# A linear-attention and mixture-of-experts kernel: rows of h scattered by expert and rank and gathered per unit, statistics and gate per unit

## The chip, the cores and the metric

The kernel runs on one core of one Trainium2 chip. A core has five engines with instruction streams of their own: TensorE (PE, matrix products), VectorE (DVE), ScalarE (ACT), GpSimd (POOL) and SyncE (SP, which here only starts DMA transfers). Each engine works its stream in order; semaphores tie the streams together. Sixteen DMA engines move data between HBM and SBUF; a transfer is started from SP's queue or, where the rows' addresses are data (indirect), from GpSimd's. The metric is the device time of one execution in microseconds.

## The reference

The input x has 2048 tokens of 512 numbers. Two blocks follow each other, each with a layer norm ahead of it and its input added to its result.

- Linear attention: q, k and v are products with wqkv; in each of 32 heads of 16, q and k go through a small matrix w_phi, and the features are softmax(p) and softmax(-p), 32 a head. With kv = phi_k^T v and z = the sum of phi_k, the output is (phi_q kv) / (phi_q z + 1e-6), times wo. So h = x + attention.
- A mixture of 8 experts, one a token: the logits are LN(h) w_gate, the largest one chooses the expert, and the token gets silu(LN(h) w1[e]) w2[e]. w1[e] is 512 x 1792, w2[e] 1792 x 512. The gate is a softmax over the one chosen logit, which is 1; both kernels compute it.

All numbers are 32-bit floats. With the given inputs the experts get 103, 594, 80, 127, 286, 222, 239 and 397 tokens.

## The kernel before, in words

**Precision.** Each large product is made of three on PE (`mm3`, L74 to L77): both operands are split into a high part (a rounded copy, by ScalarE, `hi_of`, L69) and a low part (what the rounding left, by VectorE, `lo_of`, L72). Weights are split in pieces by `split_chunk` (L170), whose subtraction (L176) goes to VectorE, or to GpSimd (`G`) where a tuple says so.

**Phase A** (`for c in range(NT - 1)`, L409) makes, per tile of 128 tokens, the layer norm, the k, q and v products, the features and the running kv. The gate's weights ride along with v and wo as extra columns, so that the logits of a tile come out of the same products; the mean is taken out afterwards with column sums of w_gate (`csg`, L366, L367, L471).

**Phase B** (`for c in range(NT + 8)`, L557) goes over the 16 tiles again, as a pipeline by hand: `s_num` (attention's quotient for tile c, L261), `s_ot` (transposed and split, c - 1), `s_wo` (output projection, residual, statistics and logits of h, c - 2), and by batches of two tiles `s_top` (the chosen expert as a one-hot row, running counts `cum`, the gate; L473), `s_rank` (each token's rank within its expert, L499) and `s_inv` (L525). h is written to a DRAM buffer `hbuf` in token order with mean, rstd and gate in extra columns (L497). `s_rank` and `s_inv` build an inverse table `ivf`: with two one-hot matrices and a product on PE (`acc`) each batch adds "token + 1" at (slot, expert and block of 128).

**Units.** A unit is 128 slots of one expert. The expert that leads after half the tokens, `star`, comes first; the others follow in order. Here that is 5 units for expert 1, then 1, 1, 1, 3, 2, 2 and 4: 19 units. In the middle of phase B `s_star` chooses the first expert and starts its seven weight chunks of 1 MB (`first_expert`, L178); when half the tokens have ranks, `s_first` reads the first unit's tokens from the table and gathers its rows (`gather`, L138). The splits of its first four chunks are laid into tiles 12 to 15 (L588), ten of sixteen low parts on GpSimd; `gemm1(0, ...)` (L594) is laid into the tail of the loop.

`unit(u)` (L719) then does: first product in four column groups (`g1`), silu, transposes and splits (`tr`), second product `g2` (14 steps into `py`), gate and residual (L797), indirect write of the rows to the output (L798). `prework(u + 1)` (L142) normalises the next unit's rows with the mean and rstd that came with them, transposes and splits them. `split(u, c)` splits a new expert's chunk under a run-time condition and then starts the load of the expert after it (`fetch`). In unit 0 stand `tables()` (L639: which unit has which expert, flags, and by `index`, L707, each unit's tokens from `ivf`), the splits of chunks 4 to 6 and the first loads for the next expert.

**What sets the order.** The source gives a priority; the framework's planner orders each engine's instructions by it and by when it expects their inputs, and may move a ready one ahead. A conditional block is moved as a whole. `issue_after` ties instructions behind a given one. So in a unit that splits, the next expert's chunks 0 to 2 are split while the unit's own first product runs, as each chunk comes free.

## Time and profile before

| | |
|---|---|
| median of 3 runs | 733.38 us (732.79 to 736.72) |
| profiled execution | 732.92 us |
| its span, first to last instruction | 731.2 us |
| VectorE / ScalarE / GpSimd busy | 468.8 / 303.2 / 180.8 us |
| DMA | 87.61 MB, mean 120 GB/s |

The span has five parts: the start to 12 us, phase A to some 205 us, phase B to some 310 us with the first unit laid into its end, the rest of the first unit to 336 us, and 18 units to 724 us, followed by the last write.

In the profile a busy time is the union of an engine's instructions. An idle time belongs to the instruction that ended it, with the instruction that released it behind the arrow. Durations of pipelined instructions overlap: where the next starts before one ends, the distance between starts is the cost. `out<-in` names what an instruction writes and reads, L is its line, x its count; "granted clock" is the share of PE's full clock.

### The profile page before, as it was taken

The numbers are of one execution on the slowest core, as the hardware profiler recorded it, in microseconds if no ns is written. First come the engines' busy times: TensorE is split into PE (matmuls) and PEld (weight loads), VectorE is DVE, ScalarE is ACT, GpSimd is POOL, SyncE is SP. The second block draws the span as 40 slices with busy tenths as digits, with TensorE's granted clock in tenths as the row PEclk, the third lists the DMA queues.
The fourth block names the chain that finished last, engine by engine and source line by source line (L and its number), as shares of the span: only waits on it lengthen the run. The fifth ranks groups of instructions, "written<-read, shape, count | busy, mean of one in ns | idle before, by whom it ended". The sixth has DMA issues, their size and how long they took to land.

```text
span 731.2 us, 12523 instructions
## 1 busy us (share of the span) xinstructions
PE 702.0 (96%) x4130; PEld 612.2 (84%) x4130; DVE 468.8 (64%) x969; ACT 303.2 (41%) x458; POOL 180.8 (25%) x281
## 2 busy tenths in 40 slices
PE   6999999999999998779999999999999999999996
PEld 6899999999989997658888888888888878888885
DVE  4996987878787889794512999972185472922211
ACT  4534444434322015152112888862274463822211
POOL 3364645434313328521110011110011111011110
PEclk9999999999999999899999999999999999999999
DMA  9111101100002249417400799981066381001000
GB/s 332 57 30 44 30 15 30 30 15 1 1 16 73 74 156 341 153 34 294 193 29 2 258 369 376 344 345 53 30 210 241 121 328 31 11 29 30 30 30 6
DMA packets 21912, 87.61 MB, mean 120 GB/s; under 512 B 3070, under 2 KB 3582, under 8 KB 14656
## 3 DMA queue, kind: packets, MB, share of 16 engines
q1 hardware_dynamic: 18624, 76.86, 28.8%
q0 software_dynamic: 3200, 9.75, 4.0%
q8 instruction: 34, 0.56, 0.3%
q14 instruction: 54, 0.44, 0.2%
HBM read 78.18 MB, written 9.21 MB: 120 GB/s over the span
## 4 chain that ended last, share of the span: by engine, by line
issue 46%; PE 35%; DMA 10%; DVE 6%; POOL 1%; ACT 1%; POOLq 1%; SPq 0%; DVEq 0%
DMA out_dram<-yo,sidx 8%; PE kvps L372 4%; PE pn L267 3%; PE pq L75 2%; PE pq L77 2%; PE pq L76 2%; PE ptq L381 2%; PE pv L77 2%; PE pv L76 2%; PE pv L75 2%; PE pk L75 2%; PE pk L77 2%; PE pk L76 2%; PE po L75 2%; PE po L76 2%
## 5 line engine op out<-in xcount | busy, mean ns | idle before, releaser
L69 ACT ACTIVATE whi<-raw 128x1024 fp32r<-128x1024 f32 (+1 forms) x120 | 118.7, 1003 | 67.9 <-PE mh L77 37.4
L176 DVE TENSOR_TENSOR wlo<-raw,whi 128x1024 fp32r<-128x1024 f32 (+1 forms) x110 | 130.6, 1200 | 18.6 <-ACT whi L69 12.5
L75 PE MATMUL mh<-whi,xhi 128*128 128x512 f32 (+1 forms) x304 | 114.9, 378 | 0.0
L77 PE MATMUL mh<-whi,xlo 128*128 128x512 f32 (+1 forms) x304 | 111.5, 367 | 0.0
L76 PE MATMUL mh<-wlo,xhi 128*128 128x512 f32 (+1 forms) x304 | 111.4, 366 | 0.0
L798 POOL DMA_INDIRECT out_dram<-yo,sidx x19 | 21.5, 1131 | 352.5 <-DVEq L635 202.0
L76 PE MATMUL my<-wlo,hThi 128*128 128x512 f32 x266 | 104.7, 393 | 3.5 <-DVE wlo L176 3.3
L75 PE MATMUL my<-whi,hThi 128*128 128x512 f32 x266 | 106.0, 399 | 0.3 <-ACT hThi L69 0.3
L77 PE MATMUL my<-whi,hTlo 128*128 128x512 f32 x266 | 104.6, 393 | 0.3 <-DVE hTlo L72 0.3
L72 DVE TENSOR_TENSOR hTlo<-mtr,hThi 128x512 fp32r<-128x512 f32 x76 | 47.0, 621 | 86.2 <-ACTq L635 53.3
L163 ACT ACTIVATE hs<-mh 128x512 f32<-128x512 f32 x76 | 41.0, 540 | 145.3 <-PE mh L77 145.3
L355 POOL TENSOR_TENSOR ph<-t,sm 128x1024 f32<-128x1024 f32 x32 | 62.1, 1939 | 66.9 <-DVE sm L353 37.8
L77 PEld LDWEIGHTS mh<-whi,xlo 128*128 128x128 f32 x304 | 57.2, 188 | 10.2
L76 PEld LDWEIGHTS mh<-wlo,xhi 128*128 128x128 f32 x304 | 57.3, 189 | 9.3
L75 PEld LDWEIGHTS mh<-whi,xhi 128*128 128x128 f32 x304 | 57.2, 188 | 9.3
L797 DVE SCALAR_TENSOR_TENSOR yo<-my,xg 128x512 f32<-128x512 f32 x19 | 14.2, 748 | 78.4 <-PE my L77 78.4
L76 PEld LDWEIGHTS my<-wlo,hThi 128*128 128x128 f32 x266 | 50.3, 189 | 14.2 <-DVE wlo L176 4.3
L77 PEld LDWEIGHTS my<-whi,hTlo 128*128 128x128 f32 x266 | 50.3, 189 | 11.2 <-DVE hTlo L72 0.5
L75 PEld LDWEIGHTS my<-whi,hThi 128*128 128x128 f32 x266 | 50.4, 189 | 10.5 <-ACT hThi L69 0.5
L352 DVE TENSOR_REDUCE sm<-t 128x64 f32<-128x1024 f32 x32 | 38.8, 1214 | 12.0 <-ACT t L347 11.9
L727 PE MATMUL mtr<-ident,hs 128*128 128x128 f32 x266 | 41.7, 274 | 2.7 <-DVE hTlo L72 2.6
L347 ACT ACTIVATE t<-t 128x1024 f32<-128x1024 f32 x32 | 33.9, 1061 | 20.9 <-DVE t L346 19.8
(206 smaller groups left out, 1407.3 us busy)
## 6 DMA issues: line engine op xcount, KB each, us to landing
raw<-in_w_dram SPq DMA_DIRECT2D x56, 1024.0 KB, 5.2
xt<-in_x_dram SPq DMA_DIRECT2D x32, 256.0 KB, 2.7
hbuf<-hb SPq DMA_DIRECT2D x8, 516.0 KB, 3.8
phT<-in_wqkT_dram SPq DMA_DIRECT2D x4, 512.0 KB, 5.1
phT<-in_wv_dram SPq DMA_DIRECT2D x2, 512.0 KB, 6.4
phT<-in_wo_dram SPq DMA_DIRECT2D x2, 512.0 KB, 8.2
phT<-in_woT_dram SPq DMA_DIRECT2D x2, 512.0 KB, 5.6
xg<-hbuf,gidx POOLq DMA_INDIRECT x21, 3.7
```

The source lines that it names most:

```text
L69: A.activation(dst, src, AF.Copy)
L72: V.tensor_tensor(dst, src, hi.bitcast(F32), op=OP.subtract)
L75: T.matmul(ps, ahi, bhi, start=first, stop=False)
L76: T.matmul(ps, ahi, blo, start=False, stop=False)
L77: T.matmul(ps, alo, bhi, start=False, stop=last)
L163: A.activation(hs[c % 2][:, 0:fw], p[:, 0:fw], AF.Silu)
L176: eng.tensor_tensor(wlo[c][:, w], raw[c][:, w], whi[c][:, w].bitcast(F32), op=OP.subtract)
L347: A.activation(t, t, AF.Exp)
L352: V.tensor_reduce(sm, t, AX.X, OP.add)
L355: G.tensor_tensor(ph.rearrange("p (a f) -> p a f", f=DH), t, bc(sm, DH), op=OP.mult)
L372: T.matmul(kvps[g // 4][:, g % 4, :], ph[:, g * P:(g + 1) * P], vt[:, 4 * g:4 * g + 4, :].rearrange("p h f -> p (h f)"), start=(c == 0 and ...
L727: T.transpose(pt[:, j * P:(j + 1) * P], hs[c % 2][:, j * P:(j + 1) * P], ident)
```

## The change

- `hbuf` has room for 2048 rows for each expert. A row holds h, the largest logit and the token's number. The running counts start at 2048 times the expert, so a token's rank is its row in `hbuf`; `s_rank` ends with that row number, and each tile is scattered from GpSimd's queue (`send`). The inverse table, `s_inv`, `index` and the one-hot matrices go. A unit's rows lie one after the other, and `gather` waits for all scatters issued before it.
- In phase A, 14 writes on SP's queue first fill all of `hbuf` with rows whose token number is out of range, so that empty slots write nothing.
- The gate's weights lose their column mean beforehand (`wgc`), so logits need no mean, and `s_wo` makes no statistics. The 1e-6 is added in halves to the two rows of z in `kvbd` (`epsz`).
- `stats(u)` makes mean, rstd and gate of a unit's rows after the gather: VectorE and GpSimd by turns. It stands after the first column group of the unit before.
- All low parts are VectorE's. The 16 pieces of chunks 0 to 3 are laid into tiles 12 to 17.
- Of the first unit only the first column group is laid ahead. Its tables are cut in two: row numbers first, so that `gather(1)` and `gather(2)` follow, flags later; the splits of chunks 4 to 6 stand between the products. Buffers of the units are allocated in another order.

```diff
-    hbuf = dram.tile([S, ROW], F32, name="hbuf")
+    hbuf = dram.tile([E * S, ROW], F32, name="hbuf")
...
+    def send(c, rows, hrow):
+        i = G.indirect_dma_start(out=hbuf, out_offset=bass.IndirectOffsetOnAxis(ap=rows, axis=0),
+                                 in_=hrow, in_offset=None)
+        for other in sent + fetched:
+            tc.declare_no_dep(i.ins, other.ins, reason="other rows of hbuf")
+        sent.append(i)
+
     def gather(u):
-        G.indirect_dma_start(out=xg[u % 3], out_offset=None, in_=hbuf if u else hbuf[0:S // 2, :],
-                             in_offset=bass.IndirectOffsetOnAxis(ap=gidx[:, u:u + 1], axis=0))
+        i = G.indirect_dma_start(out=xg[u % 3], out_offset=None, in_=hbuf,
+                                 in_offset=bass.IndirectOffsetOnAxis(ap=gidx[:, u:u + 1], axis=0))
+        for other in sent:
+            tc.add_manual_dep(i.ins, other.ins.name, mybir.DependencyInfo(
+                mybir.DependencyClass.Sync, mybir.DependencyReason.DATA), reason="rows of hbuf")
+        fetched.append(i)
+
+    def stats(u):
+        g = xg[u % 3]
+        bs = small.tile([P, 6], F32, name="ubs")
+        V.bn_stats(bs, g[:, 0:D])
+        V.bn_aggr(norm[:, u, :], bs)
+        sc = small.tile([P, 6], F32, name="usc")
+        G.tensor_scalar(sc[:, 0:1], norm[:, u, 1:2], EPS, None, op0=OP.add)
+        G.tensor_tensor(norm[:, u, 1:2], sc[:, 0:1], nhalf, op=OP.pow)
+        xi = V.tensor_scalar(xn2[0], g[:, 0:D], norm[:, u, 0:1], norm[:, u, 1:2], op0=OP.subtract, op1=OP.mult)
+        G.tensor_copy(sidx[:, u:u + 1], g[:, D + 1:D + 2])
+        V.tensor_reduce(sc[:, 1:2], g[:, D:D + 1], AX.X, OP.max)
+        G.tensor_tensor(sc[:, 2:3], g[:, D:D + 1], sc[:, 1:2], op=OP.subtract)
+        G.tensor_tensor(sc[:, 3:4], sc[:, 2:3], norm[:, u, 1:2], op=OP.mult)
+        G.tensor_tensor(sc[:, 4:5], euler, sc[:, 3:4], op=OP.pow)
+        G.tensor_scalar(sc[:, 5:6], sc[:, 4:5], 0.0, None, op0=OP.add)
+        G.tensor_tensor(sc[:, 5:6], sc[:, 5:6], mone, op=OP.pow)
+        G.tensor_tensor(gate[:, u:u + 1], sc[:, 4:5], sc[:, 5:6], op=OP.mult)
+        return xi
 
...
     def prework(u):
-        g = xg[u % 3]
-        xi = V.tensor_scalar(xn2[0], g[:, 0:D], g[:, D:D + 1], g[:, D + 1:D + 2], op0=OP.subtract, op1=OP.mult)
         pt = bank("mtr")
...
-    LO = (V,) * NW
-
-    def split_chunk(c, lo=None, n=2):
-        for i in range(n):
+    def split_chunk(c, n=2, part=None):
+        for i in range(n) if part is None else (part,):
             w = slice(i * (CW // n), (i + 1) * (CW // n))
             hi_of(whi[c][:, w], raw[c][:, w])
-            eng = lo or LO[c]
-            eng = eng[i] if isinstance(eng, tuple) else eng
-            eng.tensor_tensor(wlo[c][:, w], raw[c][:, w], whi[c][:, w].bitcast(F32), op=OP.subtract)
+            lo_of(wlo[c][:, w], raw[c][:, w], whi[c][:, w])
 
...
-        V.memset(cum[0], 0.0)
-        V.memset(ivf, 0.0)
+        G.iota(cum[0], pattern=[[S // P, E]], base=0, channel_multiplier=0, allow_small_or_imprecise_dtypes=True)
...
-                V.tensor_scalar(den, nv[:, :, DH:DH + 1], 1e-6, None, op0=OP.add)
-                V.reciprocal(den, den)
+                V.reciprocal(den, nv[:, :, DH:DH + 1])
                 V.tensor_tensor(o[:, 16 * i:16 * i + 16, :], nv[:, :, 0:DH],
...
+            V.tensor_scalar(csg, pc[:, 0:E], 1.0 / D, None, op0=OP.mult)
+            V.tensor_tensor(wgc, wgs, mid(csg, KD), op=OP.subtract)
...
+            def s_blank(c):
+                n = E * S // (NT - 2) // P
+                lo, hi = c * n * P, min((c + 1) * n * P, E * S) if c < NT - 3 else E * S
+                n = (hi - lo) // P
+                nc.sync.dma_start(hbuf[lo:hi, :].rearrange("(p r) f -> p r f", p=P),
+                                  blank.to_broadcast([P, n, ROW]))
...
-            ln_rstd(h[:, 0:D], h[:, D:D + 2], h[:, D + 1:D + 2])
-            V.scalar_tensor_tensor(lg, csg, h[:, D:D + 1], lg, op0=OP.mult, op1=OP.subtract)
...
-            G.tensor_tensor(hb[:, :, D + 2:D + 3], gt[:, 1], nr, op=OP.mult)
-            nc.sync.dma_start(hbuf[b * NB * P:(b + 1) * NB * P, :].rearrange("(c p) r -> p c r", p=P), hb)
...
-            rk = work.tile([P, NB], F32, name="rk")
-            V.tensor_reduce(rk, rs, AX.X, OP.add)
-            bs = work.tile([P, NB], F32, name="rb")
-            V.tensor_scalar(bs, rk, 0.25 - P / 2, FLOOR, op0=OP.add, op1=OP.add)
-            V.tensor_scalar(bs, bs, FLOOR, None, op0=OP.subtract)
-            sl = work.tile([P, NB], F32, name="sl")
-            V.tensor_tensor(sl, rk, bs, op=OP.subtract)
-            am = work.tile([P, NB, P], F16, name="am")
-            bm = work.tile([P, NB, E, NT], F16, name="bm")
+            to = work.tile([P, NB], F32, name="to")
+            V.tensor_reduce(to, rs, AX.X, OP.add)
+            toi = work.tile([P, NB], I32, name="toi", bufs=4)
+            V.tensor_copy(toi, to)
             for j in range(NB):
-                c = b * NB + j
-                V.tensor_scalar(am[:, j, :], iota128, sl[:, j:j + 1], None, op0=OP.is_equal)
-                jm = work.tile([P, NT], F16, name="jm")
-                V.tensor_scalar(jm, iotaS, bs[:, j:j + 1], tok1[:, c:c + 1], op0=OP.is_equal, op1=OP.mult)
-                V.tensor_tensor(bm[:, j], bc(oh[:, j, :], NT), mid(jm, E), op=OP.mult)
-            bt[b]["am"], bt[b]["bm"] = am, bm
-
-        def s_inv(b):
-            acc = pss.tile([P, P], F32, name="acc", tag="s")
-            for j in range(NB):
-                T.matmul(acc, bt[b]["am"][:, j, :], bt[b]["bm"][:, j].rearrange("p e j -> p (e j)"),
-                         start=(j == 0), stop=(j == NB - 1))
-            V.tensor_tensor(ivf, ivf, acc, op=OP.add)
+                send(b * NB + j, toi[:, j:j + 1], bt[b]["hb"][:, j, :])
 
...
-        for c in range(NT + 8):
+
+        pieces = [(i // 4, i % 4) for i in range(16)]
+        for c in range(NT + 2):
...
-                at(s_inv, b - 1, NT // NB)
                 if b == NT // NB // 2:
-                    s_first()
+                    V.tensor_scalar(gidx[:, 0:1], est, float(S), slot[:, 0:1], op0=OP.mult, op1=OP.add)
+                    gather(0)
...
-            if NT - 4 <= c < NT:
-                split_chunk(c - NT + 4, ((G, G, V, V), (G, G, G, V), (G, G, G, V), (G, G, V, V))[c - NT + 4], 4)
             if j == 0:
                 at(s_rank, b - 1, NT // NB)
+            if c == NT + 1:
+                s_top(NT // NB - 1)
+            if NT - 4 <= c < NT + 2:
+                for k in range(2 if c < NT - 2 else 3):
+                    split_chunk(pieces[0][0], 4, pieces[0][1])
+                    pieces.pop(0)
+            if c == NT - 2:
+                stats(0)
             if c == NT - 1:
                 prework(0)
-            if NT + 1 <= c <= NT + 4:
-                pre.append(gemm1(0, c - NT - 1))
-                if c <= NT + 2:
-                    silu(c - NT - 1, pre[-1])
+        pre.append(gemm1(0, 0))
+        s_rank(NT // NB - 1)
...
+        V.scalar_tensor_tensor(q, beg, float(-P), base9, op0=OP.mult, op1=OP.add)
...
+        V.scalar_tensor_tensor(rows, rows, q[:, 0:1], slot, op0=OP.add, op1=OP.add)
+        V.tensor_scalar(gidx[:, 1:NU], rows[:, 1:NU], float(E * S - 1), 0.0, op0=OP.min, op1=OP.max)
...
+        py = pss.tile([P, 512], F32, name="my", tag="s")
+        if u == 0:
+            tables1()
+            gather(1)
+            gather(2)
         g1(0)
         if u:
             split(u, 4)
+            if u + 1 < NU:
+                stats(u + 1)
+        else:
+            split_chunk(4)
         g1(1)
         tr(0)
         if u:
             split(u, 5)
+        else:
+            stats(1)
         g1(2)
         tr(1)
         if u:
             split(u, 6)
+        else:
+            split_chunk(5)
         g1(3)
         tr(2)
         if u == 0:
-            tables()
+            tr(3)
+            prework(1)
+            g2(py, 0, 4)
+            tables2()
             load_fl(0, 8)
             load_flags(0)
-        py = pss.tile([P, 512], F32, name="my", tag="s")
-        if u == 0:
-            tr(3)
-            split_chunk(4, V)
-            with after(first_[0]):
-                split_chunk(5, V)
-                g2(py, 0, 8)
-                xi = prework(1)
-            with after(xi):
-                split_chunk(6, V)
-                index(3, 4, raw[1])
+            split_chunk(6)
             for c in range(NW):
                 fetch(0, c)
             load_flags(1)
             for c in range(4):
                 split(1, c)
-            g2(py, 8, 14)
+            g2(py, 4, 14)
...
-        V.scalar_tensor_tensor(y, py, g[:, D + 2:D + 3], g[:, 0:D], op0=OP.mult, op1=OP.add)
+        V.scalar_tensor_tensor(y, py, gate[:, u:u + 1], g[:, 0:D], op0=OP.mult, op1=OP.add)
```

More of the change, by code (lines that the diff above doesn't have):

```diff
@@ L284 @@
             wgs = wp.tile([P, KD, E], F32, name="wgs")
+            blank = wp.tile([P, 1, ROW], F32, name="blank")
+            G.memset(blank, 0.0)
+            G.memset(blank[:, :, D + 1:D + 2], 2.0 * S)
             onesf = wp.tile([P, P], F32, name="onesf")
@@ L702 @@
[L702 to L717 removed]
+        live = rt.tile([P, NU], F32, name="live")
@@ new lines, in tables2 @@
+        V.tensor_scalar(live, units, end[:, EV - 1:EV], None, op0=OP.is_lt)
+        nw = rt.tile([P, NU], F32, name="nw")
+        V.memset(nw, 1.0)
+        V.tensor_tensor(nw[:, 1:NU], ex[:, 1:NU], ex[:, 0:NU - 1], op=OP.not_equal)
+        V.tensor_tensor(nw, nw, live, op=OP.mult)
+        V.tensor_copy(isnew, nw)
+        V.scalar_tensor_tensor(pick, le, 1000.0, mid(end, NU), op0=OP.mult, op1=OP.add)
+        eend = rt.tile([P, NU], F32, name="eend")
+        V.tensor_reduce(eend, pick, AX.X, OP.min)
@@ L719, in unit @@
+        V.tensor_tensor(le, mid(end, NU), bc(eend, EV), op=OP.is_le)
+        nx = rt.tile([P, NU], F32, name="nx")
+        V.tensor_reduce(nx, le, AX.X, OP.add)
+        V.tensor_scalar(nxt, nx, 1.0, float(E - 1), op0=OP.subtract, op1=OP.min)
+        V.scalar_tensor_tensor(more, nx, float(EV), nw, op0=OP.is_lt, op1=OP.mult)
     def unit(u):
```

170 lines of the change are left out of this document (63 added, 107 removed).

## The prediction

> **What bounds the kernel now.** I read the page first, then the busy time by stage, then the waits of TensorE between 275 and 338 us, then single instructions there and in a unit that changes expert.
>
> ```profile
> span 731.2 us, 12523 instructions
> ## 1 busy us (share of the span) xinstructions
> PE 702.0 (96%) x4130; PEld 612.2 (84%) x4130; DVE 468.8 (64%) x969; ACT 303.2 (41%) x458; POOL 180.8 (25%) x281
> ```
>
> TensorE (PE) is busy for 702.0 of 731.2 us. The change adds no large matmul and removes only very small ones, so what it can win lies in the 29 us of idle time and in time at a lowered clock. The profiled execution took 732.92 us, 1.7 us more than its span and 0.46 us less than the median of 733.38 us; I sum against 732.9 us. Half a percent (3.7 us) is about what a measurement of this kernel tells from no change.
>
> The next view is busy time by stage: stretch, its length, busy us of PE, weight load, VectorE, ScalarE and GpSimd, granted PE clock, DMA share, GB/s.
>
> ```profile
> 12.00:205.00 193.00, 192.32 (x1277) 175.15 (x1276) 157.66 (x256) 85.46 (x140) 85.32 (x122) 0.99 0.11 37
> 245.00:260.00 15.00, 15.00 (x136) 14.90 (x136) 13.25 (x66) 1.79 (x3) 5.07 (x14) 1.00 0.39 125
> 272.60:309.60 37.00, 29.39 (x202) 27.02 (x201) 30.87 (x111) 12.93 (x22) 25.74 (x40) 0.86 0.71 262
> 309.50:335.90 26.40, 22.33 (x110) 16.83 (x107) 24.40 (x91) 10.33 (x15) 5.39 (x10) 0.94 0.22 72
> 380.00:400.00 20.00, 20.00 (x103) 16.83 (x103) 3.56 (x6) 4.51 (x9) 1.88 (x2) 1.00 0.09 28
> 424.40:446.30 21.90, 21.53 (x110) 17.93 (x109) 20.65 (x22) 18.71 (x24) 2.72 (x2) 1.00 0.92 356
> ```
>
> The attention stage (first row), the output projection (second) and a unit that keeps its expert (fifth) are full of PE work. Three places are not. From 272.6 to 309.6 us, the last five token tiles, PE idles 7.6 us at a mean clock of 0.86. From 309.5 to 335.9 us, the first unit, it idles 4.1 us at 0.94. In a unit that fetches a new expert (last row) VectorE works 20.65 of 21.9 us, hardly less than PE.
>
> The waits of PE from 275 to 338 us (total, times, longest) say for whom it waits.
>
> ```profile
> PE my L76 <- DVE wlo L176: 3.3, 1, 3.3
> PE pl L504 <- DVE oh L483: 2.5, 1, 2.5
> PE po L75 <- DVE lg L469: 2.3, 2, 1.9
> PE pto L237 <- DVE xl L72: 2.0, 1, 2.0
> ```
>
> All four end on VectorE. Why VectorE is late there is seen in single instructions (start, duration):
>
> ```profile
> 283.27 0.28 DVE L519 TENSOR_SCALAR am<-iota,sl 128x128 f16<-128x128 f32 x1
> 283.47 0.28 DVE L522 TENSOR_TENSOR bm<-oh,jm 128x128 f16<-128x128 bf16 x1
> 283.67 1.31 DVE L519 TENSOR_SCALAR am<-iota,sl 128x128 f16<-128x128 f32 x1
> ```
> ```profile
> 283.56 3.80 POOL L176 TENSOR_TENSOR wlo<-raw,whi 128x512 fp32r<-128x512 f32 x3
> ```
>
> The same operation takes 0.28 us alone and 1.31 us once GpSimd (POOL) makes low parts beside it.
>
> **The change part by part.** *Small work removed before the units.* Groups of VectorE between 216 and 318 us (busy us, mean ns), two of GpSimd and one of PE over the whole kernel:
>
> ```profile
> L222 DVE BATCH_NORM_STATS2 bs<-hb 128x6 f32<-128x512 f32 x16 | 11.1, 694 | 0.0
> ...
> L521 DVE TENSOR_SCALAR jm<-iotaS,rb,tok 128x16 f16<-128x16 f32 x16 | 5.6, 348 | 0.0
> L519 DVE TENSOR_SCALAR am<-iota,sl 128x128 f16<-128x128 f32 x16 | 5.5, 342 | 0.0
> L522 DVE TENSOR_TENSOR bm<-oh,jm 128x128 f16<-128x128 bf16 x16 | 5.2, 328 | 0.0
> L471 DVE SCALAR_TENSOR_TENSOR lg<-csg,hb,lg 128x8 f32<-128x8 f32 x16 | 4.9, 306 | 0.0
> L176 DVE TENSOR_TENSOR wlo<-raw,whi 128x512 fp32r<-128x512 f32 x6 | 4.6, 782 | 1.8 <-ACT whi L69 1.8
> L271 DVE TENSOR_SCALAR den<-pn 128x16 f32<-128x16 f32 x26 | 4.1, 159 | 0.1
> ```
> ```profile
> L176 POOL TENSOR_TENSOR wlo<-raw,whi 128x512 fp32r<-128x512 f32 x10 | 13.0, 1328 | 1.5 <-ACT whi L69 1.5
> L226 POOL TENSOR_TENSOR hb<-ve,nhalf 128x1 f32<-128x1 f32 x16 | 9.5, 596 | 1.2
> ```
> ```profile
> L528 PE MATMUL acc<-bm,am 128*128 128x128 f16 x16 | 3.4, 226 | 0.4 <-DVE bm L522 0.4
> ```
>
> Statistics, the mean's correction, the inverse table and the 1e-6 go: 11.1 + 5.6 + 5.5 + 5.2 + 4.9 + 4.1 = 36.4 us of VectorE in eight batches, less some 0.08 us of overlap for each of 106 instructions, so about 3.5 us a batch of two tiles; the new cast gives 0.1 back. In the full stretch PE sets the pace, so this earns nothing there. The 16 acc matmuls cost 3.4 us if nothing hid them and nothing if pipelining hid them all; I take 0.6.
>
> *Low parts by VectorE alone.* Ten pieces leave GpSimd (13.0 us) for VectorE, at 0.78 us by its own row, nearer 0.6 without the collisions. VectorE's work on the last five tiles: it was busy 30.87 us; minus 2.5 batches x 3.4 = 8.5, minus some 6.5 of stretched instructions (an estimate: seven like the row of 1.31), plus 10 x 0.6 and the statistics of unit 0 (1.5): about 23 us, against 29.4 us of PE. So VectorE is still loaded but no longer late all along. The stretch loses 7.6 us by idle time and at most (1 - 0.86) x 37 = 5.2 by the clock; since part of the slow time is idle, I take 11.4 in all. The 2.0 us wait for xl, with the slow clock behind it, is a low part that waits for the first weights from HBM; nothing touches that, so 3.6 remain. Of the other 7.8 I take 5.3 and leave 2.5 for a wait of VectorE on the gather of unit 0. Bounds: 0, if VectorE stays the bound, and 11.4.
>
> *The scatter and the gather.* The eight writes on SP's queue become 16 indirect writes on GpSimd's, each behind its ranks. Landing times by group, and GpSimd's own issue times:
>
> ```profile
> hbuf<-hb SPq DMA_DIRECT2D x8, 516.0 KB, 3.8
> ...
> xg<-hbuf,gidx POOLq DMA_INDIRECT x21, 3.7
> ```
> ```profile
> 401.26 1.02 POOL L798 DMA_INDIRECT out_dram<-yo,sidx  x1 [19.08 <-DVE yo L797]
> 402.58 0.98 POOL L139 DMA_INDIRECT xg<-hbuf,gidx  x1 [0.30 <-issue]
> 425.44 1.74 POOL L798 DMA_INDIRECT out_dram<-yo,sidx  x1 [21.88 <-DVE yo L797]
> ```
>
> An issue costs 1.0 us, or 1.74 beside low parts on VectorE. GpSimd has room, since it loses the low parts. But a gather waits until every earlier scatter has landed, and behind it on GpSimd wait the operations of the statistics; VectorE stands still if its own statistics come before the rows. After the last projection (call it T0): 3 us of ranks (ten small VectorE steps; an estimate from the 0.15 to 0.35 us of the rows above), two issues 2.3, landing 3.7, gather 1.0 + 3.7, statistics 0.7 + 0.2, GpSimd's sum and power 0.3 + 0.6, normalising 0.5, transpose and split 2: unit 1 can start at T0 + 18. PE's own work until then is the first unit, 22.3 us by the row 309.5:335.9. So the chain fits with 4 us to spare, if the order puts the second product ahead of it.
>
> The Trainium skill's "SBUF — State Buffer" (section "SBUF: two separate sides") speaks against this: descriptors made on GpSimd starve while VectorE runs an operation that takes both port pairs. This trace shows 0.7 us beside low parts; by the page each of the last two scatters could wait out one VectorE operation, which the spare 4 us hide, so the sum would stay.
>
> *The first unit.* The index search (L712 and its followers), behind which chunk 5's low part stood for the 3.3 us wait, goes, and the tables are made beside the first product. The stage loses 4.1 us idle and (1 - 0.94) x 26.4 = 1.6 by the clock, 5.7 together; I let 1.7 remain, a gain of 4. Bounds: 5.7, and a loss of 1 if VectorE stands before the gather of unit 1 for 5 us.
>
> *The blank.* Phase A gets 14 writes of 2.4 MB on SP's queue, 33.7 MB, ahead of which no weight stands; the loads of x queue behind them. From 12 to 205 us the DMA is 0.11 busy at 37 GB/s, so 336 GB/s at full use: 100 us of 193. The slowest bound is the hb row, 516 KB in 3.8 us with all its latency, 136 GB/s, 248 us; then the last x tiles would come late. Three tiles are in flight and a tile takes 12 us, so I take 0; bounds 0 and 3. If this cover went, each late tile would stop VectorE and then PE.
>
> *Statistics per unit.* Each unit gets bn_stats and its fellows on VectorE, 0.6 + 0.15 + 0.1 us, a round trip to GpSimd, and the normalising earlier. In the 12 units of 19 that split nothing, VectorE has 16 us of 20 free: cost nothing. In seven units it splits a whole expert. VectorE there, and PE:
>
> ```profile
> 433.24 0.68 DVE L72 TENSOR_TENSOR hTlo<-mtr,hThi 128x512 fp32r<-128x512 f32 x1
> 433.84 0.54 DVE L144 TENSOR_SCALAR xn<-xg 128x512 f32<-128x512 f32 x1
> ...
> 435.91 1.23 DVE L176 TENSOR_TENSOR wlo<-raw,whi 128x1024 fp32r<-128x1024 f32 x1 [0.33 <-ACT whi L69]
> ```
> ```profile
> 434.07 0.41 PE L727 MATMUL mtr<-ident,hs 128*128 128x128 f32 x2 [0.37 <-DVE hTlo L72]
> ```
>
> PE already waits 0.37 us for the second hTlo, and VectorE has 0.33 us free in the whole unit. The statistics (0.85) and the moved normalising (0.45) now come before that hTlo: 1.3 us more in each of the three units that follow a unit which split too (four experts run in a row from 400 to 490 us); in the other four VectorE was idle before. 3 x 1.3 = 4 us lost. Bounds: 1.5, if 0.8 a unit falls into what xn leaves free; 12, if VectorE also waits out GpSimd's round trip (0.3 + 0.6 and the hand-over, 1.25) and the clock then takes 1.5, about what it took after the 3.3 us wait in the first unit: 3 x 4.05.
>
> On the clock, the stretch 272.6 to 309.6 shows 0.86 with idle pieces of only 2.0 and 2.5 us. The Trainium skill's "TensorE: Matmul & The Clock Gate" (Part 1) puts the drop at one idle window, about 3.4 us; by it a stall of 2 us would cost no clock, and that bound would be 7.7 in place of 12. The trace drops sooner, so the 1.5 stays in the bound; the sum is the same by both.
>
> **Sum:** 732.9 - 0.6 - 5.3 - 4.0 + 0 + 4.0 = 727.0 us.
>
> **The rivals.** (1) *The split units decide; slower.* If VectorE runs in order through the round trip, a split unit loses 1.3 + 1.25 and, with PE idle near 3 us, 1.5 by the clock: 12.2 in three units, plus 4 x 1.7 = 6.8 where only the moved work and the round trip are late: 19 against gains of 9.9, so 742. It decides from 1.4 us a split unit on. For it: 0.33 us of slack. Against it: the low parts can run during the round trip. (2) *The gather replaces the old wait; no change.* VectorE stands 4 us before unit 0's rows, whose gather shares the DMA with 4 MB of weights (share 0.71), and 5 us before unit 1's: gains 0.6 + 3.8 - 1, loss 4, so 733.5. The change then does not do what it says: VectorE is as late as before. For it: four waits in that place. Against it: GpSimd is free and rows go out two tiles early. (3) *All hidden; faster.* The stretch gains 8.9, the first unit 5, split units lose 1.5: 732.9 - 0.6 - 8.9 - 5 + 1.5 = 720.
>
> **How the numbers follow.** Forecast 0.45, (1) 0.22, (2) 0.18, (3) 0.15. Best bounds together: 732.9 - 3.4 - 11.4 - 5.7 + 1.5 = 714; worst: 732.9 + 1 + 3 + 12 = 749. The range 717 to 742 leaves out little beyond case (3)'s best and case (1)'s worst; the forecast's own is 723 to 731. Faster: 0.15 + 0.37 of the forecast's 0.45 + 0.04 of (2) = 0.56; same: 0.08 + 0.10 + 0.03 of (1) = 0.21; slower: 0.23.
>
> **What would show it.** In the changed profile: no VectorE operation of 128x128 or smaller at 1 us; PE idle from 272 to the last projection near 3 to 5 us; no 3 us wait of my for wlo; unit 1 starting near 325 us; the four dense units 23.2 us long instead of 21.9; the x loads landing without a wait of bn_stats. Wrong would be: bn_stats waiting for xg for several us, dense units over 24 us, or a PE clock under 1 in them.

## The result and the profile after

The changed kernel takes 764.75 us (median of 4 runs, 762.94 to 764.89) against 733.92 us before (4 runs, 732.79 to 736.72): ratio 1.0409, 95% interval 1.0375 to 1.0442. It is 31 us slower; the forecast was 727.0 us, in a range of 717 to 742. The profiled execution took 764.7 us.

Head of the page after:

```profile
span 763.0 us, 12461 instructions
PE 706.5 (93%) x4114; PEld 615.3 (81%) x4114; DVE 450.6 (59%) x825; ACT 303.5 (40%) x458; POOL 230.0 (30%) x360
```

VectorE (DVE) has 18 us less to do than before, as the change meant, and the kernel is longer. TensorE's busy time rose by 4.5 us though 16 small matmuls are gone: part of it ran at a lowered clock. The stages after, in the columns of the prediction's table (length, busy us of PE, weight load, VectorE, ScalarE, GpSimd, then PE clock, DMA share, GB/s):

```profile
12.00:205.00 193.00, 193.00 (x1281) 175.86 (x1280) 157.32 (x255) 87.03 (x141) 78.29 (x90) 0.99 0.72 213
272.60:303.10 30.50, 22.84 (x177) 21.75 (x177) 18.36 (x57) 10.11 (x18) 8.66 (x16) 0.89 0.60 241
303.00:330.60 27.60, 24.40 (x119) 18.81 (x119) 19.96 (x66) 10.19 (x15) 10.83 (x17) 0.94 0.24 78
423.61:453.75 30.14, 24.19 (x110) 19.85 (x109) 21.45 (x25) 18.81 (x24) 8.73 (x11) 0.89 0.69 259
```

The attention stage is as full as before, although the blank writes took the DMA share from 0.11 to 0.72. The last projection's last matmul starts 6.3 us earlier (at 302.93 us; 309.23 before), but TensorE still idles 7.7 us in them. The first unit is not shorter. And a unit that fetches a new expert right behind another such unit takes 30.14 us where it took 21.91: TensorE idle 5.95 us in place of 0.37, and 24.19 us busy in place of 21.54, at a clock of 0.89.

The waits of TensorE over the whole kernel (total, times, longest), and two of VectorE and GpSimd:

```profile
PE mtr L725 <- DVE hTlo L72: 24.3, 10, 5.5
PE mtr L182 <- DVE xn L168: 8.1, 2, 7.0
PE pf L340 <- DMA phT<-in_wqkT_dram: 6.6, 2, 5.1
PE mtr L725 <- DVEq L648: 4.4, 3, 2.9
```
```profile
DVE ubs L163 <- DMA xg<-hbuf,gidx: 66.2, 16, 6.8
...
POOL sidx L169 <- DMA xg<-hbuf,gidx: 55.0, 17, 5.6
```

Before, the kernel's only wait for gathered rows was one of 0.9 us. Now bn_stats (ubs) stands 16 times for the rows, 66 us in sum. The unit from 423.61 us shows why, in single instructions (start, duration, in brackets the idle time before and what ended it):

```profile
423.61 0.74 DVE L795 SCALAR_TENSOR_TENSOR yo<-my,gate,xg 128x512 f32<-128x512 f32 x1
...
424.64 1.84 POOL L796 DMA_INDIRECT out_dram<-yo,sidx  x1 [13.35 <-DVE yo L795]
426.79 0.98 POOL L153 DMA_INDIRECT xg<-hbuf,gidx  x1 [0.30 <-issue]
...
432.80 0.70 DVE L163 BATCH_NORM_STATS2 ubs<-xg 128x6 f32<-128x512 f32 x1 [6.18 <-DMA xg<-hbuf,gidx]
...
436.20 0.68 DVE L72 TENSOR_TENSOR hTlo<-mtr,hThi 128x512 fp32r<-128x512 f32 x1
...
437.03 1.09 PE L725 MATMUL mtr<-ident,hs 128*128 128x128 f32 x4 [5.02 <-DVE hTlo L72]
```

The gather that is issued at the start of unit u fetches the rows of unit u+2. The written order asks for the statistics of u+1 there, whose rows are a unit old; but the order of VectorE's queue is made by the planner, and it has put the statistics of u+2 in that place, directly behind the gather that fetches their rows. (One can count them: the third bn_stats, that of unit 2, which the source has in unit 1, starts at 329.69 us, ahead of unit 0's residual.) VectorE executes in order, so it stands 6.18 us; the low part hTlo, which came 5.6 us after the unit's start before, comes 12.6 us after it, and TensorE waits 5.02 and then 0.93 us.

Lengths of units, from the start of one residual operation (yo) to that of the next, in us. Units 5 to 7 each split an expert and follow a unit that did; units 4, 10, 12 and 14 split one after a unit that did not.

| kernel | start of yo, unit 0 | unit 1 | units 5, 6, 7 | units 4, 10, 12, 14 | splitting nothing |
|---|---|---|---|---|---|
| before | 336.2 | 21.4 | 21.9, 21.9, 21.9 | 24.2 | 21.3 to 21.4 |
| after | 330.6 | 25.1 | 30.1, 30.6, 30.2 | 25.2 to 25.4 | 21.4 |

Spans differ by 31.8 us: 5.6 won up to the residual of unit 0; 3.7 lost in unit 1, 25.2 in units 5 to 7, 6.4 in units 4, 10, 12 and 14 and in units 8, 11, 13 and 15, each of which comes behind a unit that splits, 0.2 in the others; 1.8 lost behind the last store (7.6 us from its issue to the end of the span, 5.8 before).

### The profile page after: what moved, and what is told of

The parts are those of the page before. It is cut to its first block, busy times and chain, and to the rows that moved or that the text cites. A ratio compares the mean times of both kernels' runs of the same rounds, so it can differ in the third digit from the quotient of the medians.

```text
span 763.0 us, 12461 instructions
## 1 busy us (share of the span) xinstructions
PE 706.5 (93%) x4114; PEld 615.3 (81%) x4114; DVE 450.6 (59%) x825; ACT 303.5 (40%) x458; POOL 230.0 (30%) x360
## 5 line engine op out<-in xcount | busy, mean ns | idle before, releaser
L72 DVE TENSOR_TENSOR wlo<-raw,whi 128x1024 fp32r<-128x1024 f32 (+1 forms) x120 | 136.1, 1150 | 22.7 <-ACT whi L69 14.9
L75 PE MATMUL my<-whi,hThi 128*128 128x512 f32 x266 | 109.2, 411 | 0.0
L77 PE MATMUL my<-whi,hTlo 128*128 128x512 f32 x266 | 106.6, 401 | 1.4 <-DVE hTlo L72 1.4
L76 PE MATMUL my<-wlo,hThi 128*128 128x512 f32 x266 | 107.1, 403 | 0.0
L796 POOL DMA_INDIRECT out_dram<-yo,sidx x19 | 23.5, 1236 | 240.8 <-DVEq L648 137.5
L72 DVE TENSOR_TENSOR hTlo<-mtr,hThi 128x512 fp32r<-128x512 f32 x76 | 47.0, 619 | 32.6 <-ACT hThi L69 21.3
L795 DVE SCALAR_TENSOR_TENSOR yo<-my,gate,xg 128x512 f32<-128x512 f32 x19 | 14.2, 749 | 85.7 <-PE my L77 85.5
L725 PEld LDWEIGHTS mtr<-ident,hs 128*128 128x128 f32 x266 | 32.5, 144 | 38.0 <-issue 19.2
L76 PEld LDWEIGHTS my<-wlo,hThi 128*128 128x128 f32 x266 | 52.1, 196 | 10.8 <-DVE wlo L72 0.4
L75 PEld LDWEIGHTS my<-whi,hThi 128*128 128x128 f32 x266 | 52.2, 196 | 10.6
L163 DVE BATCH_NORM_STATS2 ubs<-xg 128x6 f32<-128x512 f32 x20 | 13.9, 695 | 70.1 <-DMA xg<-hbuf,gidx 66.2
```

The lines of the kernel that those rows point to most:

```text
L72: V.tensor_tensor(dst, src, hi.bitcast(F32), op=OP.subtract)
L75: T.matmul(ps, ahi, bhi, start=first, stop=False)
L76: T.matmul(ps, ahi, blo, start=False, stop=False)
L77: T.matmul(ps, alo, bhi, start=False, stop=last)
L163: V.bn_stats(bs, g[:, 0:D])
L725: T.transpose(pt[:, j * P:(j + 1) * P], hs[c % 2][:, j * P:(j + 1) * P], ident)
```

## The experiments

Theory A: the loss is VectorE's wait for a gather that has only just been issued. Rival B: it is the statistics' work and their round trip to GpSimd as such. Rival C: the scatter and the gather from the larger table.

**1. Statistics at the start of the unit, of rows that are a unit old.**

```
             if u + 1 < NU:
-                stats(u + 1)
+                with tc.issue_after(done[-1].ins):   # yo of unit u-1; for u below 16
+                    stats(u + 1)
```

> The changed kernel, with the statistics of unit u+1 queued behind the residual operation of unit u-1, where the gather of their rows is a whole unit old; the work is the same. Theory A (in the changed kernel VectorE stands some 6 us at the start of each unit for a gather issued only then, and in a unit that splits an expert this holds up low parts for which PE waits): VectorE no longer waits for rows, but it now waits for GpSimd's sum and power, which stand behind two DMA issues of 1.7 to 1.8 us there, some 3.5 us in all; the three dense units take 24 to 26.5 us instead of 30.2, and the kernel 738 to 750 us. Rival B (the price is the added VectorE work and the round trip to GpSimd as such, wherever it stands): dense units of 29 to 31 us, 758 to 768 us.

Measured: 753.5 us (ratio to before 1.0279, 1.0235 to 1.0323); units 5 to 7 took 28.1, 27.7 and 27.9 us. The wait for rows is gone, and a large price stays. Unit 5 of this run (first its stretch, then VectorE and GpSimd, then TensorE):

```profile
418.80:446.86 28.06, 24.39 (x110) 19.87 (x109) 21.46 (x26) 18.72 (x24) 7.80 (x11) 0.88 0.75 278
```
```profile
421.27 0.98 POOL L153 DMA_INDIRECT xg<-hbuf,gidx  x1 [0.30 <-issue]
...
422.64 0.58 POOL L167 TENSOR_TENSOR norm<-usc,nhalf 128x1 f32<-128x1 f32 x1
...
423.25 0.55 DVE L168 TENSOR_SCALAR xn<-xg,norm 128x512 f32<-128x512 f32 x1 [2.89 <-POOL norm L167]
...
428.26 0.68 DVE L72 TENSOR_TENSOR hTlo<-mtr,hThi 128x512 fp32r<-128x512 f32 x1
```
```profile
429.09 0.63 PE L726 MATMUL mtr<-ident,hs 128*128 128x128 f32 x4 [1.86 <-DVE hTlo L72]
431.95 0.66 PE L726 MATMUL mtr<-ident,hs 128*128 128x128 f32 x2 [1.81 <-DVE hTlo L72]
```

VectorE stands 2.89 us for a power that GpSimd makes only after two DMA issues. So Rival B is not nothing: at this place the statistics' work and their round trip cost 6.2 us of unit, 3.3 more idle and 2.8 by the clock. Theory A had the direction and missed the size, since its figure had left out the clock: TensorE idled only twice, for under 2 us each.

**2. Statistics late in the unit.** The same work, for unit u+2, behind the last hTlo of unit u; the old call goes, and unit 2's statistics stand in unit 0.

```
-            tr(3)
+            last = tr(3)
+            if u + 2 < NU:
+                with tc.issue_after(last.ins):
+                    stats(u + 2)
```

> The changed kernel, with the statistics of unit u+2 queued behind the last low part of hT in unit u, 11 us or more after the issue of their gather and after GpSimd's two DMA issues; the work is the same. Theory A: no wait for rows and a round trip of 1.3 us only, hidden by the second product; dense units of 22 to 23.5 us, the unit after the first shorter by 3 us, and 726 to 736 us in all. Rival B (added work and round trip as such): dense units still of 25 us or more, 745 us or more.

Measured: 732.83 us (0.9985, 0.9963 to 1.0008); units 5 to 7: 22.2, 22.3, 22.35 us; unit 1: 21.0. Unit 5:

```profile
422.37:444.60 22.23, 21.61 (x110) 17.93 (x108) 20.73 (x26) 18.77 (x24) 8.45 (x11) 1.00 0.90 351
```
```profile
435.40 0.68 DVE L163 BATCH_NORM_STATS2 ubs<-xg 128x6 f32<-128x512 f32 x1
...
437.32 0.55 DVE L168 TENSOR_SCALAR xn<-xg,norm 128x512 f32<-128x512 f32 x1 [1.02 <-POOL norm L167]
```

The rows are there, the round trip is 1.02 us, the clock stays at 1.00. All of the statistics' work on both engines costs 0.3 to 0.4 us a unit here; the rest of the 8.2 to 8.7 was its place in the queue. (Units 4, 10, 12 and 14 are 1.0 to 1.2 us longer here too, but units 8, 11, 13 and 15 are 1.0 to 1.2 shorter than before: only the border moved.)

**3. The wait alone, in the kernel before.** No statistics, no scatter: one element a partition is copied out of the rows just being fetched.

```
+        with tc.issue_after(done[-1].ins):
+            first = V.tensor_copy(probe, xg[(u + 2) % 3][:, 0:1])
...
+        with tc.issue_after(first.ins):
             lo_of(hTlo[c], ptv, hThi[c])
```

> The kernel before with one thing added: in each unit a VectorE copy of one element a partition out of the rows that the gather at the start of that unit fetches, queued between the residual operation of the unit before and the first low part of hT. No statistics, no scatter. Theory A: VectorE stands 5 to 6 us for the rows in each unit; units that split nothing stay at 21.4 us, the three dense units go from 21.9 to 28 to 31 us, the others that split gain about 1 us each: 752 to 765 us in all. Rival B (a wait of VectorE there is hidden, the price is the statistics' work and GpSimd): dense units below 23.5 us, 734 to 740 us.

Measured: 763.68 us (1.0411, 1.037 to 1.0452); units 5 to 7: 29.6, 30.2, 30.9 us; units that split nothing 21.2 to 21.4. Unit 5, and TensorE's wait over the kernel:

```profile
437.78 0.15 DVE L728 COPY probe<-xg 128x1 f32<-128x1 f32 x1 [6.02 <-DMA xg<-hbuf,gidx]
...
440.47 0.69 DVE L72 TENSOR_TENSOR hTlo<-mtr,hThi 128x512 fp32r<-128x512 f32 x1
```
```profile
PE mtr L734 <- DVE hTlo L72: 19.3, 9, 5.5
```

A VectorE operation of 0.15 us that waits at this place, with the low parts of hT tied behind it, makes the kernel before 30 us slower, 25.0 of them in units 5 to 7. That it ends as slow as the changed kernel is in part chance: 3.0 us of this execution were lost before the first projection (table below), where the probe has no part. The gather here is from the small table, and it lands no sooner (6.02 us of waiting, 6.18 in the changed kernel). Rivals B and C are not needed for the loss of units 5 to 7.

**4. Statistics back in the attention half.** Mean, reciprocal deviation and gate travel in the row beside the token; scatter, low parts and first unit stay as changed.

```
-ROW = D + 2
+ROW = D + 4
...
             V.tensor_tensor(lg, po[:, :, D // 2:HC], xwg[:, c], op=OP.add)
+            ln_rstd(h[:, 0:D], h[:, D:D + 2], h[:, D + 1:D + 2])
...
```

> The changed kernel with one part undone: mean, reciprocal deviation and gate are again made per token tile in the attention half and carried in the row beside the token; the scatter by expert and rank, the gather, the low parts by VectorE alone and the new order of the first unit stay. Theory A: the units have no statistics to wait for, the normalising goes where it was before the change, dense units of 21.9 to 22.5 us; the last token tiles lose some of what the change won there (16 bn_stats of 0.7 us, the power on GpSimd in front of the scatters): 728 to 740 us. Rival C (the scatter and the gather from the large table, slower rows or DMA issues, are the price of the dense units): dense units still of 27 us or more, 750 us or more.

Measured: 726.47 us (0.9893, 0.9857 to 0.9929), and 726.32 us (0.9912, 0.9883 to 0.994) when it was run again beside the runs under 7:

> The kernel with the statistics back in the rows once more, beside the three runs that follow, which are compared with it: 725 to 728 us again, units that split nothing 21.3 to 21.4 us long.

All units are the old ones again (21.9 to 22.0 us, 24.2, 21.3 to 21.4), so Rival C falls for the units; and the residual of unit 0 comes at 327.3 and 324.8 us, 8.9 and 11.4 us earlier than before (2.2 of the 11.4 were there at the first projection, which starts at 208.5 us in the second run, 210.6 in the first and 210.7 before). The change without its statistics per unit is worth about 8 us, and these, as they were queued, cost 38.

**5. Low parts back to GpSimd**, in the kernel of 4.

```
-                    split_chunk(pieces[0][0], 4, pieces[0][1])
+                    split_chunk(pieces[0][0], 4, pieces[0][1], lo)   # lo: G for 10 pieces, V for 6
```

> The kernel with the statistics back in the rows (726.5 us), and another part of the change undone: ten of the sixteen pieces of the first expert's low parts go back to GpSimd, as before the change. If leaving them to VectorE alone is what makes the last token tiles shorter: GpSimd's scatters and its powers come later by up to 13 us of low parts and VectorE's small operations stretch again, 730 to 738 us. Rival (the tiles got shorter by the statistics and tables that went, and VectorE is as loaded with the low parts as without): 724 to 728 us.

Measured: 737.01 us (1.0036, 1.0015 to 1.0057), some 10.6 us more than without. GpSimd's groups from 270 to 330 us, and TensorE's waits from 264 to 340 us:

```profile
L193 POOL TENSOR_TENSOR wlo<-raw,whi 128x512 fp32r<-128x512 f32 x10 | 13.2, 1342 | 0.0
L146 POOL DMA_INDIRECT hbuf<-hb,toi x10 | 10.3, 1035 | 2.8 <-issue 1.7 <-POOL hb L524 0.5 <-DVE lg L498 0.2
```
```profile
PE mtr L169 <- DVE xn L166: 4.5, 1, 4.5
PE my L77 <- DVE hTlo L72: 3.1, 1, 3.1
PE pl L531 <- DVE oh L511: 3.0, 2, 1.6
```

The ten low parts stand among scatters that others wait for. With the scatter on GpSimd's queue, leaving it the low parts makes the kernel slower than before, so this part of the change is what lets the scatter pay; whether by the scatters held up or by VectorE's stretched operations, the run doesn't separate. The units are unchanged (21.9 to 22.0).

**6. The last token tiles.** In the changed kernel TensorE's 7 us wait there is for the first unit's normalised rows:

```profile
278.09 0.99 POOL L153 DMA_INDIRECT xg<-hbuf,gidx  x1 [8.22 <-DMA hbuf<-hb,toi]
...
285.00 0.69 DVE L163 BATCH_NORM_STATS2 ubs<-xg 128x6 f32<-128x512 f32 x1 [3.53 <-DMA xg<-hbuf,gidx]
...
291.28 0.19 POOL L505 COPY hb<-tok 128x2 f32<-128x2 f32 x1 [3.27 <-DMA hbuf<-hb,toi]
...
292.02 0.57 POOL L167 TENSOR_TENSOR norm<-usc,nhalf 128x1 f32<-128x1 f32 x1
...
292.63 0.55 DVE L168 TENSOR_SCALAR xn<-xg,norm 128x512 f32<-128x512 f32 x1 [6.47 <-POOL norm L167]
```

The sum and the power of 0.8 us stand on GpSimd behind two scatters and a copy that waits for a scatter. The run ties that copy behind the power.

```
-                G.tensor_copy(bt[b]["hb"][:, :, D + 1], tok[:, c:c + NB])
+                with tc.issue_after(first[0]) if first else ExitStack():   # first: the power of unit 0
+                    G.tensor_copy(bt[b]["hb"][:, :, D + 1], tok[:, c:c + NB])
```

> The changed kernel with one copy moved on GpSimd: the copy of the token numbers into the last row buffer, which waits 3.3 us for a scatter to land, is queued behind the power of the first unit's statistics instead of ahead of it. Theory A for the last token tiles (TensorE's 7 us wait there is VectorE standing for the power, and the power stands behind that copy): the wait of 6.5 us of VectorE for the power falls to 2.5 to 3.5 us, TensorE's wait for the first unit's normalised rows from 7.0 to 3 to 4 us, the kernel 759 to 763 us. Rival (the wait is the gather's landing and the low parts; the copy's wait only moves to VectorE's write into the same buffer): TensorE still waits 6 us or more, 763 to 766 us.

Measured: 760.71 us (1.0354, 1.03 to 1.0409). From 264 us on, VectorE and TensorE:

```profile
DVE xn L170 <- POOL norm L167: 3.1, 1, 3.1
```
```profile
PE mtr L184 <- DVE xn L170: 6.1, 2, 3.7
```

VectorE's wait for the power fell from 6.47 to 3.10 us and TensorE's in the last tiles from 7.05 to 3.7, as expected; the other wait of the second row, 2.4 us, lies in the first unit, where it was 1.1. The intervals of this run and of the changed kernel overlap, so the 4 us of the medians rest on these rows more than on the times.

**7. The tiles of the second product's weights.** In the kernel of 4 the first unit still waits: the low part of chunk 4 is written where the last scatters still read, 6.9 us of VectorE and 5.0 of TensorE (310.1 to 315.1 us), with the clock at half for the 10 us from 310 to 320, the wait among them:

```profile
DVE wlo L72 <- DMA hbuf<-hb,toi: 6.9, 1, 6.9
...
PE my L77 <- DVE hTlo L72: 5.0, 1, 5.0
```
```profile
310.00:320.00 10.00, 5.04 (x13) 3.88 (x13) 7.94 (x11) 2.29 (x4) 3.09 (x5) 0.50 0.26 81
```

Three layouts of the same tiles in the unit stage, the first two with chunk 6 in that place:

```
 e6_rows_buffers:  hThi hTlo whi4 xhi1 xlo1 xg2 yo whi6 wlo6 wlo4 whi5 wlo5
 e6b_rows_buffers: hThi hTlo whi4 xhi1 xlo1 yo whi6 wlo6 wlo4 whi5 wlo5 xg2
 e11_shift:        16 bytes, then as in the changed kernel
```

> The kernel with the statistics back in the rows (the run before, 726.5 us), and the tiles of the second product's weights laid out in another order, so that the low part of chunk 4 no longer lies over the row buffers that the last scatters still read; chunk 6 does. There VectorE stood 6.9 us for a scatter's landing, with the low parts of hT behind it, and TensorE 5.0 us, with its clock at 0.50 for the next 10 us. If that wait is what the first unit still loses: TensorE waits under 2 us there, clock 1.00, 718 to 723 us. Rival (the first unit has to wait for the last scatter and the gather behind it anyway, so the wait only moves to the rows of the second unit): 724 to 727 us.

Measured: 728.55 us (0.9928, 0.9907 to 0.9949), against 726.5: no gain, and outside both forecasts. TensorE's 5.0 us wait is gone, and 2.7 us for the rows of unit 1 take its place; the residual of unit 0 comes at 326.2 us. But every unit is about 0.2 us longer, 21.5 to 21.6 us. Unit 2 of this run, which splits nothing (groups of TensorE: busy us, mean ns), and then unit 2 with the layout e6b:

```profile
L75 PE MATMUL my<-whi,hThi 128*128 128x512 f32 x14 | 5.6, 400 | 0.0
L76 PE MATMUL my<-wlo,hThi 128*128 128x512 f32 x14 | 5.5, 396 | 0.0
L77 PE MATMUL my<-whi,hTlo 128*128 128x512 f32 x14 | 5.5, 393 | 0.0
```
```profile
L75 PE MATMUL my<-whi,hThi 128*128 128x512 f32 x14 | 5.5, 396 | 0.0
L76 PE MATMUL my<-wlo,hThi 128*128 128x512 f32 x14 | 5.5, 391 | 0.0
L77 PE MATMUL my<-whi,hTlo 128*128 128x512 f32 x14 | 5.5, 390 | 0.0
```

Three to five ns more in each of 42 matmuls make most of the 0.2 us. The next two runs ask whether a shift in bytes does it.

> The kernel with the statistics back in the rows (726.5 us), with nothing but an unused tile of 16 bytes a partition ahead of the tiles of the unit stage, so that all of these move by 16 bytes. In the run with the other layout the matmuls of the second product took 394 to 399 ns instead of 390 to 395, and a unit 0.2 us more; there an odd-sized row buffer (2064 bytes) had come ahead of the weights. If the shift by 16 bytes is the cause: units of 21.5 to 21.6 us, 729 to 731 us. Rival (which tile lies where, not its byte offset, or no cause of the layout at all): 21.3 to 21.4 us, 725 to 728 us.

> The layout of the run of 728.55 us, with the odd-sized row buffer behind all weights, so that chunk 4 still avoids the row buffers and no weight is shifted by 16 bytes. If the shift cost the 0.2 us a unit: units of 21.3 to 21.4 us, the first unit 1 us shorter than with the old layout, 723.5 to 726 us. Rival (the place of the tiles): 727.5 to 730 us.

The shift by 16 bytes gave 726.93 us (0.9911, 0.9886 to 0.9937), units of 21.3 to 21.4: no effect. With the odd-sized row buffer behind the weights the time is 723.95 us (0.9873, 0.9848 to 0.9898), units of 21.3 to 21.4, the residual of unit 0 at 324.0 us. So it isn't the byte offset of all tiles; a row buffer of 2064 bytes between hT and most of the weights goes with the loss, and why stays open (hT and weights were not shifted against each other alone; in the kernel before, that buffer lay ahead of both). Run e6b has the lowest median of the study; its interval lies below that of e6 and overlaps those of the kernel of 4 (0.9857 to 0.9929 and 0.9883 to 0.994).

**8. Statistics per unit, with all three moves** (2, 6 and the layouts of 7).

> The changed kernel with statistics still per unit and three moves together: statistics of unit u+2 behind the last low part of hT in unit u (732.8 us alone), the token copy behind the first power, the new layout of the second product's weights. If the waits add up as their traces show (3.5 us of TensorE at the last tiles, 2 us in the first unit): 726 to 730 us. If the last tiles and the first unit only pass the wait on to the next one: 731 to 734 us.

> Statistics per unit, moved behind the last low part of hT, with the token copy behind the first power (731.2 us with the first new layout), now with the layout that keeps the odd-sized row buffer behind all weights. If the shift cost 0.2 us a unit: units that split nothing of 21.3 to 21.4 us, 726 to 729 us; otherwise 730 to 733 us.

Measured: 731.24 us (0.999, 0.9963 to 1.0017) with the layout of e6, units of 21.5 to 21.6; 727.17 us (0.9919, 0.9893 to 0.9946) with that of e6b, units of 21.4. The first is the less hopeful of its two cases by the time, but every unit carries the 0.2 us of that layout, so it doesn't tell whether a wait was passed on; the second came as forecast. Statistics per unit can be had for a gain of 0.5 to 1.1% on the kernel before, 3 us behind the version that carries them in the rows.

| kernel | us | first projection | yo of unit 0 | unit 1 | units 5, 6, 7 |
|---|---|---|---|---|---|
| old rows (1) | 753.5 | 211.9 | 329.6 | 21.0 | 28.1, 27.7, 27.9 |
| late statistics (2) | 732.8 | 210.7 | 333.4 | 21.0 | 22.2, 22.3, 22.35 |
| before + wait (3) | 763.7 | 213.7 | 339.9 | 21.9 | 29.6, 30.2, 30.9 |
| statistics in rows (4) | 726.5 | 210.6 | 327.3 | 21.4 | 21.95, 21.9, 21.9 |
| low parts to GpSimd (5) | 737.0 | 212.4 | 339.6 | 21.4 | 21.95, 21.9, 22.0 |
| layout e6b (7) | 724.0 | 209.6 | 324.0 | 20.8 | 22.0, 21.9, 21.95 |
| all in units, layout e6b (8) | 727.2 | 208.3 | 327.1 | 21.0 | 22.25, 22.3, 22.35 |

The first projection starts at 210.7 us before and 210.6 after. It differs between two profiles of one kernel too (210.6 and 208.5 us for that of 4), so two starts of yo are best compared from there.

## Why the prediction was wrong

The step that failed is *Statistics per unit*, in the sentence that each unit gets bn_stats and its fellows and "the normalising earlier", priced at 1.3 us in three units by their durations alone. It never asked whose rows stand there. The diff writes statistics of u+1, and I took the queue to follow it, though the profile before held the warning: in that kernel the normalising of rows fetched in the same unit already stood in the unit of their gather, with no wait only because it came late: at 433.84 us in the prediction's rows, 9.4 us after the unit's start. An operation that the planner pulls a unit ahead, and that now comes early in the unit, meets the gather in flight. bn_stats waiting for xg for several us was the prediction's own first sign of being wrong, and it came. The term measured 25.2 us in units 5 to 7, 6.4 around the other four and 3.7 in unit 1, in place of 4.0; its upper bound of 12 held only the round trip.

Point by point:

- *In the 12 units that split nothing: no cost* was right where such a unit follows one like it: these stay at 21.4 us, though VectorE waits 5.1 us for rows in units 2 and 3 too. Unit 1, and units 8 and 13 behind units that split, grew by 3.7, 0.6 and 1.3 us.
- *Rival (1)* had the place and the sign (split units, in-order VectorE, the clock behind it), with the wrong mechanism: it charged a round trip of 1.25 us and 1.5 by the clock, 4.05 a unit. Run 1 has that round trip: with two DMA issues ahead of the power, it and the work cost 6.2 us in unit 5. In the changed kernel the rows stood in its place: after 6.18 us for them, VectorE did other work until the normalising at 439.67 us, which waited for nothing. The rival's 0.33 us of slack counted the one wait alone; by the prediction's row VectorE was not busy for 1.25 us of that unit.
- *Low parts by VectorE alone* had the mechanism: the stretched operations are gone (the 16 low parts of the first expert took 0.68 us each), and run 5 puts its worth at some 10.6 us on top of the scatter. Its size in the changed kernel came out smaller than the 6.3 us by which the last projection ends earlier: 1.6 us were won before the twelfth tile's projection (272.22 us, 273.81 before), and six large matmuls of the first unit, some 1.4 us, now come behind the last projection instead of ahead of it. That leaves about 3.3 us for a forecast of 5.3.
- *The 2.5 us left for the gather of unit 0* was too little: 3.5 us for the rows and 6.5 for the power, seen from VectorE. That is rival (2)'s mechanism, and run 6 takes 3.4 of the power's wait away.
- *The first unit's 4.0* did not come in the changed kernel (27.4 us from the last projection to the residual, 26.7 before). TensorE's idle time there fell only from 4.1 to 3.2 us: the 3.3 us wait for a low part went, and waits of 1.4, 1.1 and 0.7 us came, the first because VectorE stood 1.9 us before a weight's low part, for a scatter that still read the place it is written to; the prediction had not looked at what the new tiles lie over. And TensorE does more in the stretch, eleven large matmuls of a first product, 0.23 us apart: the six just named, and five more of unit 1 that run before the residual.
- *The blank at 0* was right at a DMA share of 0.72; the attention stage kept TensorE full.
- *The acc matmuls* were not measured alone.

Taken without the statistics, the sum was 723.0 us, and the versions that carry these in the rows run at 726.5 and 724.0. That this is so near is partly luck: these versions make the statistics in the tiles again, 11.1 us of VectorE that the sum had taken out, and where their gain lies was forecast only in part.

The Trainium skill's "TensorE: Matmul & The Clock Gate" (Part 1) puts the drop to half clock at one idle window of about 3.4 us. The prediction kept a clock price against it, and run 1 bears that out, though the price was 2.8 us and not 1.5: two idle pieces of 1.86 and 1.81 us, with 1.0 us of matmuls between, brought the clock to half. TensorE's stretches of 1 us there (columns as above):

```profile
430.00:431.00 1.00, 0.15 (x2) 0.00 (x0) 1.00 (x2) 0.83 (x2) 0.00 (x0) 0.87 0.99 418
431.00:432.00 1.00, 0.04 (x1) 0.08 (x2) 1.00 (x3) 0.00 (x0) 0.00 (x0) 0.50 0.99 418
...
437.00:438.00 1.00, 1.00 (x4) 0.74 (x4) 0.53 (x1) 0.24 (x1) 0.00 (x0) 0.72 0.00 0
```

## What to carry to other kernels

When a change adds a reader of fetched data to an in-order engine, find in the queue as it is issued, not in the source, which fetch it stands behind; a planner may pull it one step ahead, next to the issue. A wait of 5 us cost nothing in a unit with slack, and one of 6 cost over 8 us in a unit where that engine is full, so price it in the full units, and add the clock. Tie such a reader behind the last operation that the bound engine waits for.

## What was not expected of the hardware

- The clock. In run 1 two waits of 1.9 and 1.8 us, 1 us apart, cost 2.8 us beyond the 3.7 us of idle time: it was down from about 430.7 to 437.6 us, and TensorE was busy for 5.6 of these 6.8 us, at half speed. In unit 5 of the changed kernel it was down from about 436.5 to 443.4 us, 6.8 us again, with 5.4 busy and 2.65 lost. In the clock records of all fourteen traces, each stretch at half clock before the last matmul lasts 3.41, 6.83 or 10.24 us, one, two or three times 3.41, and nothing between.
- GpSimd's small operations stretch beside VectorE's low parts of weights. In the changed kernel the power of one column took 0.57 us in the last tiles (row 292.02 above) and 1.47 us in unit 5, where VectorE makes such low parts from 433.92 to 436.28 us:

```profile
434.12 1.47 POOL L167 TENSOR_TENSOR norm<-usc,nhalf 128x1 f32<-128x1 f32 x1
```

  Of its 20 executions 7 took 1.45 to 1.58 us, all of them beside low parts of weights, whose two inputs are in SBUF. The other 13 took 0.57 or 0.58, several of them beside low parts of hT, which have one input in PSUM. The Trainium skill's "SBUF — State Buffer" (section "Who interferes with whom") says that a VectorE instruction with two inputs from SBUF contends with a GpSimd instruction that reads SBUF, which agrees. It also says that such an operation did not hold up descriptors made on GpSimd. The traces don't settle that: beside low parts of weights an output write's issue took 1.84 us (424.64 in the changed kernel) against 1.0 to 1.1 us otherwise, but a gather's issue beside them took 0.98 us in the kernel before (427.49) and 1.81 in run 2 (425.55). So the prediction's 1.74 us beside low parts holds for the write alone.
- 33.7 MB of blank writes beside the attention stage, at a DMA share of 0.72, cost TensorE nothing that shows.
- Behind the issue of the last store the span goes on for 7.6 us in the changed kernel, 7.5 to 7.6 in every run with the scatter, and 5.8 us in the two without; what takes the 1.8 us doesn't show in the trace.
